# Memory's sums in 116 columns, six low halves on GpSimd, and a new order, in a gated attention and feed-forward kernel

## The chip, the cores and the metric

The kernel runs on one core of a Trainium2 chip. The metric is device time in microseconds (us), the median of several executions. The engines are TensorE (PE in the profile, its weight loads PEld), VectorE (DVE), ScalarE (ACT), GpSimd (POOL), and SyncE (SP), whose queue issues most transfers.

## The reference

One input `x` of 2048 tokens by 448 features goes through two branches that share it, and a gate mixes them:

```python
g = _sigmoid((x * gate_w).sum(-1, keepdims=True))
a = _A_ref(x, A_wq, A_wk, A_wv, A_wo, A_beta)
b = _B_ref(x, B_w1, B_w2)          # silu(x @ w1) @ w2, 448 -> 1792 -> 448
return g * a + (1 - g) * b
```

Branch A is attention with 16 heads of 28 features in four segments of 512 tokens. Inside a segment it is ordinary causal attention. Across segments there is a memory, a 28 x 28 matrix M and a vector z for each head:

```python
for s in range(N):
    qs, ks, vs = q[:, :, s], k[:, :, s], v[:, :, s]
    ...                             # a_dot: causal softmax attention
    pq = phi(qs)                    # phi(t) = t + 1 if t > 0 else exp(t)
    num = jnp.einsum("bhld,bhde->bhle", pq, M)
    den = jnp.einsum("bhld,bhd->bhl", pq, z)[..., None] + 1e-6
    o = g * num / den + (1.0 - g) * a_dot
    pk = phi(ks)
    M = M + jnp.einsum("bhld,bhle->bhde", pk, vs)
    z = z + jnp.einsum("bhld->bhd", pk)
```

## The kernel before

**Precision.** Matmuls run on 16-bit numbers, but every operand is kept as two halves: a high half (the scaled value rounded to 16 bits) and a low half (the scaled value less the high one). A product takes three matmuls: high by high, high by low, low by high. The high half is mostly made by ACT (L603), the low half by `rest`: one DVE instruction (L592), or two POOL instructions (L594 scales in place, L595 subtracts).

**Stages.** `project()` covers about the first 155 us. It loads x and the weights, finds scales, splits x and the weights into halves, makes queries, keys (`proj`) and values (`vproj`) for 16 groups `t` (segment `s`, four heads `g` each), and builds and reads the memory (`memory`, `retrieve`). Attention (`attention`) and a first pass of the feed-forward branch (ten of 14 blocks) follow together; the second pass and the output projection end the kernel. The queries and keys go through DRAM (`q_scr`, `k_scr`) and come back as `ring`.

**x's halves.** `xhalves(s, c, prio)` makes both halves of segment `s`'s chunk `c`: four chunks of features, the last one with 64 rows. For the first segment DVE makes the low halves. For the others the planner chooses DVE or POOL; in the profile all of them are on DVE.

**Memory.** There are 12 units: `memory(t, ...)` for segments 0 to 2. PE adds, over four blocks of 128 tokens, phi(k)'s halves by v's halves in one PSUM tile: the first matmul (L1046) takes phi(k)'s high half by both halves of v, 232 columns; the second (L1048) phi(k)'s low half by v's high half, 116 columns. DVE adds the two column sets together (L1057, into `md`). POOL multiplies by `bds` (L1060), which holds scales and zeros where a key's head isn't the value's, and, from segment 1 on, adds into `macc` (L1062). ACT and POOL split `macc` into `mhl` (L1065, L1066), which `retrieve` uses as a matmul operand (L1083, L1084) for the next segment.

**Scales.** After the scale of a segment's x is known (`top`, `up`), POOL makes a chain of small operations: `true` and `kscale`, then `others`, which makes `bds` (`PREADY`) and then the scales of the scores (`EREADY`).

**Order.** `tc.manual_schedule()` is on, and the order of all instructions comes from a planner written in the kernel (`Sched`). Every task has an engine (or two to choose from), an estimated duration, dependencies, buffers that it takes, and a priority. The planner lets the tasks run in its own model, always the one that can start first, and among those that can start at the same time the one with the lowest priority number; that fixes each engine's program. For PE, `price` adds a cost for weight loads that wouldn't be hidden. Group `t` of the projections has priority 10 t in `project()`; attention's head `n` has 10 n, and the feed-forward's first pass is spread from `FLO` to `FHI`. About 45 constants shift these priorities: `OT1` places `others`, `SS` a segment's x halves, `MP` memory, `FIRST` and `MAXO` the first attention group, `WPRIO` and `XPRIO` the feed-forward's weights and scales, `WOT` and `WOP` the output projection, `LOP` the low halves of attention's weights. `few(n, ...)` tells the planner that a POOL task takes 0.33 n us. `MORE` is the number of extra warm-up matmuls that PE may run when it has nothing else (L816).

Of the kernel before, what the change touches and what calls it, by code (L numbers as in the profile page):

```python
# [14 lines left out]
OP = mybir.AluOpType  # L15
AX = mybir.AxisListType
# [4 lines left out]
GW = 4 * DH  # L21
# [5 lines left out]
TB = L // 128  # L27
SCALE = DH ** -0.5
LIFT = 8.0 * math.log(2.0)
TALL = 2.0 ** 15  # L30
NEG = -1.0e30
NT = NSEG * NG
NH = NT * 4
NA = 5
COLD = 5.0
WARM = 8
MORE = 4
HPRIO = 30.66
BANKS = {"mm": 3, "sc": 3, "cc": 2}
FREE = FB - 1  # L40
PASSES = [list(range(0, 10)), list(range(10, FB))]
# [3 lines left out]
DOWN = 2.0 ** -19  # L45
TINY = 2.0 ** -40
FIT = 2.0 ** -15
WOT = 286.86
TUS = 1.6
TLAT = 4.0  # L50
SLACK = -0.5
LOP = 75.43
LATE = -0.33
FIRST = 111.83
WPRIO = 120.5
MAXO = 65.16
FULL = 0.111
LOCK = 0.06
RB = "cc"
MP = 26.33  # L60
VF = -48.01
VA = 10.9
VS = 2.57
NV = 8
XH0 = -43.53
NF = 4
VE = 6.87
LASTQ = 5.78
WQS = -110.77
VH = 48.29  # L70
XS0 = -70.23
VC = -7.5
OT1 = -83.52
XS = 36.84
QS = -38.93
KS1 = -37.16
SS = -17.65


def VP(o, k):  # L80
    return o + VA + VS * k if o or k > VF else -1.0 + 0.1 * k


PRICE = 303.25
PRICE2 = 1.93
SLACK2 = 0.6
PVRUNS = [((1, 0), 1)]
PVP = 47.73
FLO = 57.98
FHI = 686.35  # L90
WOP = 120.98
SZ = 17.27
SZSTEP = -0.26
XPRIO = 311.22
WBP = 41.87
XLEAD = 146.82


# [180 lines left out]
def infini_mix(ctx: ExitStack, tc: tile.TileContext, x, wq, wk, wv, wo, beta, w1, w2, out):  # L279
    nc = tc.nc  # L280
# [39 lines left out]
    def half(cols, n=1):  # L320
        return [(0.0025 + cols * 0.000418, 0.027)] * n
# [15 lines left out]
    def dve(cols, fn, *deps, **k):  # L337
        return sch.add("DVE", 0.07 + 0.00104 * cols, fn, deps, **k)
# [4 lines left out]
    def pool(cols, fn, *deps, **k):  # L343
        return sch.add("POOL", 0.1 + 0.0019 * cols, fn, deps, **k)
# [33 lines left out]
    WV, WQ, HQ, WK, HK, W1, W2, WO, NS = range(NSEG, NSEG + 9)  # L378
# [50 lines left out]
    SIZE, SQUARED, SCALED, XH, JUNK = {}, {}, {}, {}, []  # L429
# [92 lines left out]
    def few(n, fn, *deps, **k):  # L522
        return sch.add("POOL", 0.33 * n, fn, deps, port=None, **k)
# [26 lines left out]
    def others(s, prio, bds, own, t_own, t_gh):  # L550

        def mem():
            z = spk[:, NSEG + s:NSEG + s + 1]
            by(z, top[:, WK:WK + 1], top[:, xi(s)], 1.0 / FIT)
            by(z, z, 1.0 / UP, op0=OP.max)
            by(bds[:, s, :, DH:], own[:, :, None], z[:GW])
            by(bds[:, s, :, :DH], own[:, :, None].to_broadcast([GW, 4, DH]), z[:GW], rv[:GW, s:s + 1])

        def go():
            by(rv[:, s:s + 1], top[:, WV:WV + 1], top[:, xi(s)], 1.0 / FIT)  # L560
            by(omgs[:, s], omg, rv[:, s:s + 1])
# [12 lines left out]
        EREADY[s] = few(8, scores, PREADY[s], SCALED[WQ], SCALED[WK], prio=prio + 0.5)  # L574
        END1.append(EREADY[s])

    DER = {}
# [188 lines left out]
    def project():  # L766
# [82 lines left out]
        def xhalves(s, c, prio):  # L849
            ALL, END = slice(None), slice(REM, 128)  # L850
            b, d = XR.pop((s, c))
            if s == 0:
                sl = slice(c * 128, (c + 1) * 128)
                hi = (ALL, slice(0, 4), sl)
                lo = [((ALL, slice(4, 7), sl), (ALL, slice(0, 3)), (ALL, slice(0, 3), sl)),
                      ((END, NC, sl), (END, NC), (END, NC, sl))]

                def src():
                    return b.v.rearrange("p (c n) -> p c n", c=4)
            else:  # L860
                hi = (ALL, c)
                lo = [((ALL, 4 + c), (ALL,), (ALL, c)) if c < NC else ((END, NC), (END,), (END, NC))]

                def src():
                    return b.v
            XC[s, c] = halves(NSEG - 1 - s, hi, lo, lambda: X16[s], src, L, d, prio, uses=[b], both=s == 0,
                              on="DVE" if s == 0 else None)
            XH.setdefault(s, []).extend(XC[s, c])

        XC, EARLY = {}, {}  # L870
# [164 lines left out]
        def memory(t, prio):  # L1035
            s, g = divmod(t, NG)
            b, done = PK.pop(t)
            ps = Buf(BK["cc"])
            vs = [VB[s * TB + tb] for tb in range(TB)]

            def go():
                p = ps.v[:GW, :2 * (GW + 4)]
                q = p.rearrange("p (h t e) -> p h t e", h=4, t=2)
                for tb in range(TB):
                    vv = vs[tb][0].v[:, 4 * g:4 * g + 4]
                    nc.tensor.matmul(p, b.v[:, 0, tb], vv.rearrange("p h t e -> p (h t e)"), start=(tb == 0), stop=False,  # L1046
                                     skip_group_check=True)
                    nc.tensor.matmul(q[:, :, 0], b.v[:, 1, tb], vv[:, :, 0], start=False, stop=(tb == TB - 1),  # L1048
                                     skip_group_check=True)
            m = pe((half(232) + half(116)) * TB, go, *done, *[d for v in vs for d in v[1]], takes=[ps],  # L1050
                   uses=[b] + [v[0] for v in vs], prio=prio)
            ma = macc[:, g].rearrange("p (h e) -> p h e", h=4)
            d = Buf(R["md"])

            def red():
                p = ps.v[:GW, :2 * (GW + 4)].rearrange("p (h t e) -> p h e t", h=4, t=2)
                nc.vector.tensor_reduce(d.v, p, axis=AX.X, op=OP.add)  # L1057

            def acc():
                nc.gpsimd.tensor_mul(ma if s == 0 else d.v, d.v, bds[:, s])  # L1060
# [46 lines left out]
        for i in range(4):  # L1107
            b = Buf(WAR)
# [412 lines left out]
```

## Time and profile before

| | |
|---|---|
| median of 3 runs | 550.92 us (549.62 to 553.25) |
| the profiled execution | 551.97 us |
| its span, first to last instruction | 550.0 us |
| mean granted clock of TensorE | 0.997 |
| bytes moved by DMA | 78.93 MB |

The profile is of one execution. Its page gives busy times by engine and the chain of work that ended last. Other views group instructions by line, list them in time, or give the busy time of each engine in a stretch of time. A row of the timeline has its start, its duration (or the stretch from the first to the last of several), engine, line, operation, output and inputs, shape and count; what stands in brackets is the idle time of that engine before it and what ended it. A matmul's duration in a row is its whole way through the array; how often a new one starts tells what it costs.

### The profile page before, as it was taken

What the parts mean: (1) busy time and instruction counts of PE and PEld (TensorE: products, weight loads), DVE (VectorE), ACT (ScalarE), POOL (GpSimd) and SP (SyncE); (2) the same over time, 40 slices, a digit from 0 to 9 for tenths busy, and PEclk for the clock granted to TensorE, in tenths of its full rate; (3) what the DMA queues carried; (4) which work ended last, traced back from release to release, by engine and by line L of the source; (5) the groups of instructions that cost most, each with busy time, mean ns of one, the idle gap of its engine ahead of it and who ended that gap; (6) DMA issues with size and microseconds to landing.
All of it is one profiled execution on the core that took longest, in us unless ns stands there. A gap on an engine that the chain in (4) does not pass through costs nothing.

```text
span 550.0 us, 11589 instructions
## 1 busy us (share of the span) xinstructions
PE 538.9 (98%) x4027; PEld 299.0 (54%) x4027; DVE 409.7 (74%) x1003; ACT 408.0 (74%) x698; POOL 357.6 (65%) x551
## 2 busy tenths in 40 slices
PE   8999999999998999999999999999999999999997
PEld 3445556665634555555565556565555555555544
DVE  4999899988759877598665889877888137654473
ACT  5978899687347988899887998889999897410140
POOL 3356353676515878998799998899889996122210
PEclk9999999999999899999999999999999999999999
DMA  8769786346457242432324334356402222699872
GB/s 277 257 201 247 225 241 202 129 118 200 144 161 199 80 113 72 150 88 70 85 86 120 87 89 122 103 137 179 81 12 65 86 69 65 228 243 240 235 163 73
DMA packets 78058, 78.93 MB, mean 144 GB/s; under 512 B 44168, under 2 KB 67720, under 8 KB 78000
## 3 DMA queue, kind: packets, MB, share of 16 engines
q1 hardware_dynamic: 77424, 77.21, 49.2%
q10 hardware_dynamic: 576, 0.99, 0.6%
q8 instruction: 31, 0.51, 0.4%
q14 instruction: 27, 0.22, 0.2%
HBM read 48.41 MB, written 26.09 MB: 135 GB/s over the span
## 4 chain that ended last, share of the span: by engine, by line
PE 84%; DMA 5%; DVE 5%; ACT 3%; issue 1%; SPq 1%; POOL 0%; DVEq 0%; ACTq 0%; POOLq 0%
PE mm L629 23%; PE mm L1235 17%; PE sc L629 10%; PE sc L734 6%; PE sc L1331 6%; PE cc L1365 6%; PE cc L1235 6%; PE cc L629 5%; DMA rawf<-in_w_dram 2%; PE sc L992 2%; DMA raw<-in_wv_dram 1%; ACT pf L1336 1%; PE cc L1083 1%; DMA ring<-k_scr 1%; DMA xraw<-in_x_dram 1%
## 5 line engine op out<-in xcount | busy, mean ns | idle before, releaser
L1352 POOL TENSOR_TENSOR phl<-pf,phl 128x384 f16<-128x384 f32 (+1 forms) x192 | 187.3, 997 | 14.6 <-ACT phl L1348 13.7
L1336 ACT ACTIVATE pf<-sc,lift,es 128x512 f32<-128x512 f32 (+1 forms) x192 | 125.9, 708 | 8.9 <-PE sc L1331 8.0
L747 DVE CUSTOM_DVE_ANT_0 sc<-sc,mk 128x384 f32<-128x384 f32 (+1 forms) x192 | 105.2, 572 | 25.6 <-PE sc L734 22.4
L1235 PE MATMUL mm<-wb,ghl 128*128 128x448 f16 (+2 forms) x516 | 112.6, 348 | 0.2 <-DVE wb L592 0.2
L629 PE MATMUL mm<-xh,wa 128*128 128x512 f16 x429 | 108.2, 378 | 0.0
L1235 PEld LDWEIGHTS <-ghl 128*128 128x128 f16 x684 | 63.9, 97 | 51.9 <-issue 0.8
L1348 ACT ACTIVATE phl<-pf 128x1280 f16<-128x1280 f32 x64 | 80.8, 1272 | 12.0 <-POOL pf L1342 11.5
L629 PEld LDWEIGHTS <-wa 128*128 128x128 f16 x572 | 54.0, 98 | 55.7 <-issue 3.8
L1331 PE MATMUL sc<-ring 86*128 86x512 f16 (+3 forms) x256 | 61.9, 300 | 0.2
L734 PE MATMUL sc<-ring 84*128 84x128 f16 (+3 forms) x256 | 59.4, 300 | 2.4 <-DMA ring<-k_scr 1.4
L1373 DVE TENSOR_REDUCE oraw<-cc 128x116 f32<-128x232 f32 x64 | 25.3, 395 | 28.8 <-PE cc L1365 28.6
L1365 PEld LDWEIGHTS <-phl 128*128 128x128 f16 x1280 | 41.4, 96 | 8.9
L1365 PE MATMUL cc<-vg,phl 128*128 128x29 f16 (+1 forms) x1280 | 43.6, 182 | 0.0
L629 PE MATMUL mm<-xh,wks 128*128 128x512 f16 x176 | 43.0, 380 | 0.4 <-DVE stg L934 0.4
L640 POOL TENSOR_TENSOR ol<-ol,ml 128x448 f32<-128x448 f32 x12 | 14.1, 1172 | 44.5 <-DMA ol<-o_scr 25.1
L629 PE MATMUL mm<-xh,wqs 128*128 128x512 f16 x176 | 42.0, 379 | 0.4 <-DVE vt L1016 0.4
L629 PE MATMUL cc<-xh,wa 128*128 128x512 f16 x143 | 37.7, 389 | 0.6 <-DVE amr L1089 0.4
L1235 PE MATMUL cc<-wb,ghl 128*128 128x448 f16 x168 | 38.2, 352 | 0.0
L1342 POOL TENSOR_SCALAR_AFFINE_SELECT pf<-pf 128x384 f32<-128x384 f32 x64 | 33.7, 527 | 6.6 <-ACT pf L1336 6.0
L646 ACT ACTIVATE oh<-ol,os 128x448 f16<-128x448 f32 x16 | 10.7, 666 | 34.7 <-POOL ol L640 34.7
L1331 PEld LDWEIGHTS <-ring 86*128 86x128 f16 x256 | 24.0, 97 | 22.7 <-issue 1.5
L629 PE MATMUL sc<-wos,oT 128*128 128x448 f16 x176 | 35.4, 352 | 0.0
(190 smaller groups left out, 943.0 us busy)
## 6 DMA issues: line engine op xcount, KB each, us to landing
rawf<-in_w_dram SPq DMA_DIRECT2D x26, 256.0 KB
rawf<-in_w_dram SPq DMA_DIRECT2D x28, 224.0 KB
v_scr<-vt SPq DMA_DIRECT2D x16, 232.0 KB
vg<-v_scr SPq DMA_DIRECT2D x16, 232.0 KB
xraw<-in_x_dram SPq DMA_DIRECT2D x14, 256.0 KB
q_scr<-stg SPq DMA_DIRECT2D x16, 224.0 KB
ring<-q_scr SPq DMA_DIRECT2D x16, 224.0 KB
k_scr<-stg SPq DMA_DIRECT2D x16, 224.0 KB
```

What stands on the lines that cost most here:

```text
L629: nc.tensor.matmul(ps(), *p[i], start=(i == 0), stop=(i == n - 1))
L640: d = pool(530, lambda: nc.gpsimd.tensor_add(b.v, b.v, m.v), d, e, uses=[b, m], **k)
L734: nc.tensor.matmul(ps.v[:, u:u + n], rg.v[:KS, 0, hh, i * 128:(i + 1) * 128], rg.v[:KS, 1, hh, :n], start=i + t > 0, stop=(i + t > 0 or j ...
L747: nc.vector.tensor_tensor_reduce(r, r, MK[:, L - n:], 1.0, NEG, OP.add, OP.max, mx.v[:, hh, i:i + 1])
L1235: nc.tensor.matmul(ps.v[:, lo:hi], g.v[:, y, sl], w.v[:, z, lo:hi], start=(j == 0 and i == 0), stop=(j == len(fs) - 1 and i == 2))
L1331: nc.tensor.matmul(ps.v[:, e:e + w], rg.v[:KK, 1, hh, j * 128:(j + 1) * 128], rg.v[:KK, 0, hh, j * 128:], start=True, stop=True)
L1336: ex.append(sact(e, lambda b=b, ps=ps, pf=pf, e=e: nc.scalar.activation(pf.v[:, b, :e], ps.v[:, :e], AF.Exp, bias=lift, scale=es[:, s:s + ...
L1342: mk.append(pool(204, lambda pf=pf: nc.gpsimd.affine_select(pf.v[:, :, :128], pf.v[:, :, :128], [[0, 3], [1, 128]], OP.is_ge, 0.0, base=0, ...
L1348: hi = copy(1280, lambda hl=hl, flat=flat: nc.scalar.activation(hl.v[:, 0], flat(), AF.Copy), *mk, takes=[hl], uses=[pf], prio=p0 + 2)
L1352: low = pool(w - u + 22, lambda hl=hl, flat=flat, u=u, w=w: nc.gpsimd.tensor_sub(hl.v[:, 1, u:w], flat()[:, u:w], hl.v[:, 0, u:w]), low, u ...
L1365: nc.tensor.matmul(p[:, i, :2 - z], hl.v[:, z, u:u + 128], vg.v[:, j, hh, :2 - z], start=(z == zs[0] and i == 0), stop=(z == zs[-1] and j ...
L1373: nc.vector.tensor_reduce(orw.v[:, hh], p, axis=AX.X, op=OP.add)
```

## The change

Three things are changed, and the planner's constants with them.

1. `memory`: three matmuls of 116 columns for each block of tokens, all into the same 116 columns of PSUM, take the place of one of 232 and one of 116. DVE multiplies that sum, read from PSUM, by `bds`; there is no reduction, and POOL's multiplication is gone. For segment 0 DVE writes `macc` itself; later POOL adds `md` into it.
2. `xhalves`: for segments 1 to 3 the low halves of chunks 0 and 2 are made by POOL, in two instructions each. For chunks 1 and 3 the planner still chooses.
3. `MORE` goes from 4 to 6, and the planner's estimate of the last scale operations from 8 to 10 units of 0.33 us.

```diff
+AWAY = (0, 2)
...
-MORE = 4
-HPRIO = 30.66
+MORE = 6
+HPRIO = 11.4
...
-WOT = 286.86
+WOT = 458.77
...
-LOP = 75.43
-LATE = -0.33
-FIRST = 111.83
-WPRIO = 120.5
-MAXO = 65.16
+LOP = 190.26
+LATE = -0.25
+FIRST = 169.25
+WPRIO = 82.91
+MAXO = 73.19
...
-MP = 26.33
+MP = 23.77
...
-OT1 = -83.52
...
-SS = -17.65
+OT1 = -132.99
...
+SS = -14.27
...
-PRICE2 = 1.93
-SLACK2 = 0.6
+PRICE2 = 250.34
+SLACK2 = -0.07
...
-FLO = 57.98
-FHI = 686.35
-WOP = 120.98
+FLO = 15.0
+FHI = 718.21
+WOP = 60.65
...
-XPRIO = 311.22
-WBP = 41.87
+XPRIO = 190.9
+WBP = 14.98
...
-        EREADY[s] = few(8, scores, PREADY[s], SCALED[WQ], SCALED[WK], prio=prio + 0.5)
+        EREADY[s] = few(10, scores, PREADY[s], SCALED[WQ], SCALED[WK], prio=prio + 0.5)
...
-                              on="DVE" if s == 0 else None)
+                              on="DVE" if s == 0 else "POOL" if c in AWAY else None)
...
             def go():
-                p = ps.v[:GW, :2 * (GW + 4)]
-                q = p.rearrange("p (h t e) -> p h t e", h=4, t=2)
+                p = ps.v[:GW, :GW + 4].rearrange("p (h e) -> p h e", h=4)
                 for tb in range(TB):
                     vv = vs[tb][0].v[:, 4 * g:4 * g + 4]
-                    nc.tensor.matmul(p, b.v[:, 0, tb], vv.rearrange("p h t e -> p (h t e)"), start=(tb == 0), stop=False,
-                                     skip_group_check=True)
-                    nc.tensor.matmul(q[:, :, 0], b.v[:, 1, tb], vv[:, :, 0], start=False, stop=(tb == TB - 1),
-                                     skip_group_check=True)
-            m = pe((half(232) + half(116)) * TB, go, *done, *[d for v in vs for d in v[1]], takes=[ps],
+                    for i, (y, z) in enumerate(((0, 0), (0, 1), (1, 0))):
+                        nc.tensor.matmul(p, b.v[:, y, tb], vv[:, :, z], start=tb + i == 0, stop=tb == TB - 1 and i == 2)
+            m = pe(half(116) * 3 * TB, go, *done, *[d for v in vs for d in v[1]], takes=[ps],
                    uses=[b] + [v[0] for v in vs], prio=prio)
             ma = macc[:, g].rearrange("p (h e) -> p h e", h=4)
             d = Buf(R["md"])
 
-            def red():
-                p = ps.v[:GW, :2 * (GW + 4)].rearrange("p (h t e) -> p h e t", h=4, t=2)
-                nc.vector.tensor_reduce(d.v, p, axis=AX.X, op=OP.add)
-
-            def acc():
-                nc.gpsimd.tensor_mul(ma if s == 0 else d.v, d.v, bds[:, s])
-                if s > 0:
-                    nc.gpsimd.tensor_add(ma, ma, d.v)
-            r = dve(227, red, m, takes=[d], uses=[ps], prio=prio)
-            r = pool(156 if s == 0 else 423, acc, r, PREADY[s], *MH.get((s - 1, g), []), uses=[d], prio=prio)
+            def mul():
+                p = ps.v[:GW, :GW + 4].rearrange("p (h e) -> p h e", h=4)
+                nc.vector.tensor_mul(ma if s == 0 else d.v, p, bds[:, s])
+            r = dve(150, mul, m, PREADY[s], *(MH.get((s - 1, g), []) if s == 0 else []), takes=[d] if s else [], uses=[ps], prio=prio)
+            if s:
+                r = pool(156, lambda: nc.gpsimd.tensor_add(ma, ma, d.v), r, *MH.get((s - 1, g), []), uses=[d], prio=prio)
```

The constants left out of this diff move in the same way: `XH0`, `VF`, `VA`, `VS`, `VE`, `VH`, `LASTQ`, `WQS`, `XS0`, `XS`, `QS`, `KS1`, `PRICE`, `PVP`, `SZ` and `SZSTEP`.

More of the change, by code (lines that the diff above doesn't have):

```diff
@@ L59 @@
 RB = "cc"
-MP = 26.33
-VF = -48.01
-VA = 10.9
-VS = 2.57
+MP = 23.77
+VF = -58.98
+VA = 12.89
+VS = 2.6
 NV = 8
-XH0 = -43.53
+XH0 = -65.85
 NF = 4
[L67 to L71, printed above, removed]
-VC = -7.5
-OT1 = -83.52
-XS = 36.84
-QS = -38.93
-KS1 = -37.16
-SS = -17.65
+VE = 6.88
+LASTQ = 5.69
+WQS = -96.81
+VH = 16.89
+XS0 = -38.95
+VC = -7.5
+OT1 = -132.99
+XS = 34.38
+QS = -42.27
+KS1 = -18.8
+SS = -14.27
 def VP(o, k):
     return o + VA + VS * k if o or k > VF else -1.0 + 0.1 * k
-PRICE = 303.25
-PRICE2 = 1.93
-SLACK2 = 0.6
+PRICE = 290.47
+PRICE2 = 250.34
+SLACK2 = -0.07
 PVRUNS = [((1, 0), 1)]
-PVP = 47.73
-FLO = 57.98
-FHI = 686.35
-WOP = 120.98
-SZ = 17.27
-SZSTEP = -0.26
-XPRIO = 311.22
-WBP = 41.87
+PVP = 49.52
+FLO = 15.0
+FHI = 718.21
+WOP = 60.65
+SZ = 11.47
+SZSTEP = 0.05
+XPRIO = 190.9
+WBP = 14.98
 XLEAD = 146.82
```

## The prediction

> **What bounds the kernel now.** I read the page first: its busy times, and the shares of the chain that ended last. After it the busy times by stretch, then the timeline of each engine where the edits lie.
>
> ```profile
> span 550.0 us, 11589 instructions
> ...
> PE 538.9 (98%) x4027; PEld 299.0 (54%) x4027; DVE 409.7 (74%) x1003; ACT 408.0 (74%) x698; POOL 357.6 (65%) x551
> ...
> PE 84%; DMA 5%; DVE 5%; ACT 3%; issue 1%; SPq 1%; POOL 0%; DVEq 0%; ACTq 0%; POOLq 0%
> ```
>
> TensorE (PE) is busy for all but 550.0 - 538.9 = 11.1 us, and 84% of the chain is its own work. Whatever the other engines save is worth only what it takes out of these 11.1 us, plus what it takes out of a slowed clock. Where do they lie? In the view by stretch the columns are PE, PEld, DVE, ACT, POOL, granted clock, DMA share and GB/s:
>
> ```profile
> 20.00:40.00 20.00, 19.16 (x89) 8.48 (x88) 19.76 (x40) 16.13 (x36) 8.82 (x13) 1.00 0.70 213
> 40.00:60.00 20.00, 19.92 (x126) 11.77 (x124) 19.51 (x37) 16.25 (x42) 10.75 (x27) 1.00 0.89 246
> ...
> 160.00:180.00 20.00, 17.24 (x84) 7.78 (x83) 15.77 (x39) 13.57 (x23) 8.64 (x10) 0.95 0.69 185
> 180.00:200.00 20.00, 19.90 (x176) 11.06 (x175) 16.16 (x43) 18.94 (x29) 16.27 (x23) 0.96 0.28 76
> ```
>
> The handover from the projections to attention (160 to 200) holds 2.76 + 0.10 = 2.86 us of idle PE, and a granted clock of 0.95 and 0.96 there, worth another 20 x 0.05 + 20 x 0.04 = 1.8 us. From 20 to 60 us VectorE (DVE) is busy for 39.27 of 40 us beside an almost full PE. So DVE is the second bound just where the edits fall, and GpSimd (POOL), at 19.57 of 40 us, has room.
>
> **The change part by part.** The profiled execution took 551.97 us with its span of 550.0, so 1.97 us lie around the span; the median of the runs shown is 550.92, 1.05 lower. I make the sum on 551.97 and carry it over to the median with that difference.
>
> *Memory's matmuls.* There are 12 units of four blocks. A block was one matmul of 232 columns and one of 116; now it is three of 116. Start to start in the PE timeline gives their price:
>
> ```profile
> 42.42 0.26 PE L1046 MATMUL cc<-vt,phk 128*112 128x232 f16 x1
> 42.52 0.22 PE L1048 MATMUL cc<-vt,phk 128*112 128x116 f16 x1
> 42.57 0.26 PE L1046 MATMUL cc<-vt,phk 128*112 128x232 f16 x1
> ```
>
> The 232 columns take 0.10 us (42.42 to 42.52), the 116 take 0.05 (42.52 to 42.57): 0.15 us a block before, 3 x 0.05 = 0.15 after. The rows are rounded to 0.01 us, so three of them may be 0.015 off either way, times 48 blocks: 0 +- 0.7 us. I take +0.2.
>
> *Two more warm-up matmuls (MORE 4 to 6).* Two of the four run just ahead of the row at 5.81, two at 20.65 in the same timeline:
>
> ```profile
> 5.81 0.99 PE L992 MATMUL sc<-raw,xraw 128*128 128x450 f32 x2 [0.95 <-DMA xraw<-in_x_dram]
> ...
> 20.65 0.60 PE L816 MATMUL mm<-maskb 128*128 128x512 bf16 x2
> 21.09 4.91 PE L629 MATMUL mm<-xh,wqs 128*128 128x512 f16 x22
> ```
>
> Such a matmul costs (21.09 - 20.65) / 2 = 0.22 us. In the 0.95 us of idle PE ahead of 5.81 two of them cost nothing; at 20.65, in front of the first projection, they cost 0.44. I take the middle, +0.2.
>
> *Memory's sums.* The reduction on DVE and the masking on POOL become one multiplication on DVE that reads PSUM.
>
> ```profile
> L1057 DVE TENSOR_REDUCE md<-cc x12: 383/390/394, 45.0 to 143.1; 112x116 f32<-112x232 f32 x12
> L1060 POOL TENSOR_TENSOR md<-md,bds x8: 428/433/878, 80.6 to 143.6; 112x116 f32<-112x116 f32 x8
> ```
>
> ```profile
> L759 DVE SCALAR_TENSOR_TENSOR mhl<-sc,mhl x16: 268/274/279, 98.4 to 431.2; 16x128 f16<-16x128 f32 x16
> ```
>
> The new operation is in no row. From above the old reduction of twice the columns bounds it (0.390 us), from below the nearest DVE row with one input in PSUM and one in SBUF (0.274 for 128 columns); I take 0.27, since the row's size is almost the same. DVE gains 12 x 0.12 = 1.4 us, POOL 12 x 0.43 = 5.2 us. A wait is added: DVE's multiplication now waits for POOL's mask (bds), and behind it in DVE's order stand the second halves of projections (stg), which free PE's banks. The first mask is ready at 42.64 (row 42.21 below) and the first reduction ran at 45.0, so this wait is covered by 2.4 us, if POOL makes the mask no later.
>
> *Low halves of x's chunks 0 and 2, segments 1 to 3.* Six of the nine full DVE operations go to POOL, which needs two passes for each.
>
> ```profile
> L592 DVE SCALAR_TENSOR_TENSOR xh<-xraw,up,xh 128x512 f16<-128x512 f32 x9 | 6.3, 744 | 0.0
> ```
>
> ```profile
> 169.92 1.57 POOL L594 TENSOR_SCALAR rawf<-rawf,up 128x512 f32<-128x512 f32 x1
> 171.57 1.15 POOL L595 TENSOR_TENSOR wa<-rawf,wa 128x512 f16<-128x512 f32 x1
> ```
>
> DVE gains 6 x 0.744 = 4.5 us; POOL pays 6 x (1.57 + 1.15) = 16.3 us. POOL's sum is then 357.6 + 16.3 - 5.2 = 368.7 us, still no bound as a sum. What matters is when PE asks for these halves. For segment 1 (PE, then ACT, then POOL):
>
> ```profile
> 43.03 0.73 PE L629 MATMUL sc<-wvs,xh 128*128 128x450 f16 x3
> ...
> 45.27 1.69 PE L629 MATMUL sc<-wvs,xh 128*128 128x450 f16 x8
> ```
>
> ```profile
> 36.96 0.72 ACT L603 ACTIVATE xh<-xraw,up 128x512 f16<-128x512 f32 x1
> ```
>
> ```profile
> 42.21 0.43 POOL L529 TENSOR_SCALAR bds<-of,spk,rv 112x112 f32<-112x112 f32 x1
> ...
> 49.19 0.22 POOL L527 TENSOR_SCALAR wide<-wide 128x1 f32<-128x1 f32 x1
> ```
>
> Chunk 0's high half ends at 37.68. If POOL takes both low halves at once, they end at 37.7 + 2.72 = 40.4 and 43.1. PE asks for chunk 0 at 43.03 and for chunk 2 only within the eight matmuls from 45.27: nothing is lost. If they stand behind the first mask (42.64), they end at 45.4 and 48.1, and PE is 2.4 us late. If they stand behind the whole chain of small scale operations (to 49.41), see the rival. Between the first two I take half, +1.2. For segment 2:
>
> ```profile
> 68.92 2.85 DVE L592 SCALAR_TENSOR_TENSOR xh<-xraw,up,xh 128x512 f16<-128x512 f32 x4
> ```
>
> ```profile
> 80.35 0.81 PE L629 MATMUL mm<-xh,wqs 128*128 128x512 f16 x3
> ```
>
> DVE was done at 71.77 and the query projection first asks at 80.35: 8.6 us of cover, which holds even 3 x 2.72 us of POOL. I cost it at nothing; the cover is gone only if POOL starts after 74.9.
>
> *What DVE's 5.9 us can buy.* Of PE's waits in the stretch, DVE ended three:
>
> ```profile
> 26.36 2.54 PE L629 MATMUL mm<-xh,wqs 128*128 128x512 f16 x11 [0.35 <-DVE vt L1016]
> ...
> 29.96 4.91 PE L629 MATMUL mm<-xh,wks 128*128 128x512 f16 x22 [0.42 <-DVE stg L934]
> ...
> 66.74 0.73 PE L629 MATMUL sc<-wvs,xh 128*128 128x450 f16 x3 [0.40 <-DVE vt L1016]
> ```
>
> Together 0.35 + 0.42 + 0.40 = 1.17 us; the first two lie ahead of every operation that is taken from DVE. So between 0 and 1.17 is gained; I take -0.5.
>
> *The redrawn order.* About forty constants of the planner move the places of nearly all work, and the profile shows none of it. Downward it can win no more than the handover and those waits (2.86 + 1.8 + 1.17 = 5.8); upward, one more place like the handover costs 4.7. I take 0 and keep both ends.
>
> Sum: 0.2 + 0.2 + 1.2 - 0.5 + 0 = +1.1, so the profiled execution would take 551.97 + 1.1 = 553.1 us, and the median 1.05 less: 552.0 us. The rivals below are priced from the median at once.
>
> *A rule on the port.* In this trace DVE and POOL hold each other up. One DVE operation of the low-half kind took 1.59 us while POOL was in its subtractions:
>
> ```profile
> 217.62 1.59 DVE L592 SCALAR_TENSOR_TENSOR wb<-rawf,up,wb 128x448 f16<-128x448 f32 x1
> ```
>
> ```profile
> 216.70 2.03 POOL L1352 TENSOR_TENSOR phl<-pf,phl 128x384 f16<-128x384 f32 x2
> ```
>
> ```profile
> L592 DVE SCALAR_TENSOR_TENSOR wb<-rawf,up,wb x12: 672/735/1646, 175.5 to 460.4; 128x448 f16<-128x448 f32 x12
> ```
>
> The median of its kind is 0.735 and the longest 1.646, so one meeting costs up to 0.91 us. The Trainium skill, "SBUF — State Buffer", section "Who interferes with whom", says that a DVE instruction with two SBUF inputs and a GpSimd instruction that reads SBUF exclude each other, the second waiting until the first is through; the rows agree. It speaks against this change: twelve new POOL passes read SBUF beside a DVE that is full. What that would make of the time is the third rival.
>
> **The rivals.**
>
> *Faster: the handover closes.* With 5.9 us less on DVE the projections end earlier, and the new order has no wait and no slow clock at 160 to 200. For it: DVE's 39.27 of 40 us. Against it: that handover shows a DVE that is busy only 15.77 of 20 us, so it is not DVE that it lacks. It gives 550.9 - 5.8 = 545.1 us.
>
> *Slower: POOL's order.* The place is segment 1's chunk 0. If POOL runs its chain of small operations first, to 49.41, chunk 0's low half ends at 49.41 + 2.72 = 52.1, against the 43.03 at which PE asks: 9.1 us. PE's work from 43.60 to 45.27 can go ahead of it, 1.7 us, which leaves 7.4. It decides from the point where chunk 0's low half ends after 43.03 + 1.7 = 44.7. For it: the planner gives most of that chain the better priority (segment 1's part of it stands at 40 + OT1 = 40 - 132.99 = -93, the halves at 30 + SS = 16, and the lower goes first). Against it: the planner sees the same durations and would price such a wait. It gives 550.9 + 0.4 + 7.4 = 558.7.
>
> *Slower: the port.* If each of the twelve POOL passes meets a DVE operation with two SBUF inputs, DVE loses 12 x 0.91 = 10.9 us against 5.9 gained, 5.0 net, in stretches where it has no slack; with the 2.4 us of lateness above, 550.9 + 0.4 + 7.4 = 558.7 as well. For it: the row of 1.59 us. Against it: most DVE operations there read PSUM or a single tile.
>
> **How the numbers follow.** Forecast 0.43, handover closes 0.20, POOL's order 0.22, port 0.15. About 1%, 5.5 us, is what a measurement of this kernel can tell from no change: the within-1% band is 545.4 to 556.4, and the forecast with its unknowns (-5.8 to +4.7 around 552.0) lies in it but for its ends. So faster 0.20, same 0.43, slower 0.37. The forecast's own range is 547 to 556. The range for 8 in 10 goes from 544.5, just under the faster rival, to 561, the slower ones with the uncertain 2 us of their sums.
>
> **What would show it.** Memory's three matmuls: start to start 0.05 us. DVE's multiplication: 0.27 us, no reduction left. POOL's low halves: 2.7 us a chunk, and their end against the first PE operation on segment 1. DVE's busy time from 20 to 110 us some 4 to 6 us lower. The port: DVE operations on L592, or those that read two tiles, over 1 us beside POOL's passes. The handover: idle PE and granted clock at 160 to 200. I am wrong if PE idles over 3 us near 43 us, or if the idle time at the handover is under 1 or over 6 us.

## The result, and the profile after

| | median | range | n | ratio to before [95% interval] |
|---|---|---|---|---|
| before | 551.71 us | 549.62 to 556.52 | 13 | |
| after | 548.79 us | 548.16 to 550.68 | 13 | 0.9949 [0.9928, 0.9970] |

The changed kernel is 0.5% faster, between 0.3% and 0.7%: 2.9 us where the prediction's sum had +1.1. The page after, its span, busy times and chain of waits:

```profile
span 547.0 us, 11704 instructions
...
PE 538.3 (98%) x4077; PEld 300.0 (55%) x4077; DVE 408.4 (75%) x1004; ACT 406.7 (74%) x696; POOL 359.4 (66%) x543
...
PE 86%; ACT 5%; DMA 4%; DVE 2%; issue 1%; SPq 1%; DVEq 0%; ACTq 0%
```

PE's idle time fell from 11.1 to 547.0 - 538.3 = 8.7 us. DVE's sum fell by 1.3 us only, although 5.9 us of work were taken from it: the planner put other work there, in part what POOL had (two low halves of the weights `wvs` and two sums `hsum`, 1.35 and 1.84 us on DVE). By stretch, with the columns of before:

```profile
20.00:40.00 20.00, 20.00 (x100) 9.69 (x100) 19.76 (x42) 16.49 (x37) 4.55 (x8) 1.00 0.81 253
40.00:60.00 20.00, 19.66 (x120) 10.86 (x119) 18.45 (x35) 18.98 (x47) 18.66 (x32) 1.00 0.87 256
160.00:180.00 20.00, 17.10 (x86) 8.02 (x84) 17.83 (x47) 13.52 (x21) 10.52 (x12) 0.91 0.56 153
180.00:200.00 20.00, 19.71 (x198) 11.54 (x196) 18.07 (x46) 19.21 (x32) 16.26 (x24) 1.00 0.33 95
```

From 20 to 40 us PE has no idle time left, and POOL is now nearly full from 40 to 60. The handover is as it was: 2.90 + 0.29 us of idle PE. Over the stretches ahead of it, before and then after:

```profile
0.00:20.00 20.00, 17.85 (x49) 7.66 (x50) 11.99 (x48) 13.35 (x36) 5.96 (x31) 1.00 0.85 280
20.00:150.00 130.00, 128.22 (x753) 74.26 (x752) 119.19 (x250) 99.72 (x221) 71.12 (x144) 1.00 0.65 193
```

```profile
0.00:20.00 20.00, 18.96 (x51) 7.76 (x52) 12.77 (x49) 14.44 (x38) 6.13 (x31) 1.00 0.80 283
20.00:150.00 130.00, 129.66 (x811) 75.78 (x811) 116.78 (x252) 99.46 (x220) 79.28 (x142) 1.00 0.65 195
```

PE's idle time falls from 2.15 to 1.04 us up to 20 us, and from 1.78 to 0.34 us from 20 to 150. (A second profile of before, *before_again* below, has 1.56 and 1.64.) The first feed-forward matmul, before and then after:

```profile
150.93 2.32 PE L629 MATMUL cc<-xh,wa 128*128 128x512 f16 x10 [0.37 <-DVE amr L1089]
```

```profile
148.46 2.54 PE L630 MATMUL cc<-xh,wa 128*128 128x512 f16 x11
```

The first of attention's scores come 20.45 us after it in before (171.38) and 20.55 us after it in the changed kernel (169.01). So in these profiles 2.4 of the 3.0 us by which the span is shorter are gained in the projections, ahead of the handover. The edits themselves, in the timelines of PE and POOL and in the rows of DVE's line:

```profile
42.79 0.81 PE L1047 MATMUL cc<-vt,phk 128*112 128x116 f16 x12
43.44 0.81 PE L630 MATMUL mm<-xh,wqs 128*128 128x512 f16 x3
44.09 2.26 PE L630 MATMUL sc<-wvs,xh 128*128 128x450 f16 x11
```

```profile
39.02 1.57 POOL L595 TENSOR_SCALAR xraw<-xraw,up 128x512 f32<-128x512 f32 x1 [0.72 <-ACT xh L604]
40.67 1.16 POOL L596 TENSOR_TENSOR xh<-xraw,xh 128x512 f16<-128x512 f32 x1
...
44.76 1.58 POOL L595 TENSOR_SCALAR xraw<-xraw,up 128x512 f32<-128x512 f32 x1
46.43 1.16 POOL L596 TENSOR_TENSOR xh<-xraw,xh 128x512 f16<-128x512 f32 x1
```

```profile
L1055 DVE TENSOR_TENSOR md<-cc,bds x8: 259/270/279, 75.5 to 136.5; 112x116 f32<-112x116 f32 x8
```

Twelve matmuls of 116 columns take 43.44 - 42.79 = 0.65 us. Chunk 0's low half of segment 1 ends at 41.83, PE asks for it at 44.09. DVE's multiplication takes 0.27 us. So each edit does what it says, at the forecast price. The rows show where PE waits less, but not which of the edits, or the new order, did it.

### The profile page after: what moved, and what is told of

Read it like the earlier page. It is cut to its first block, busy times and chain, and to the rows that moved or that the text cites. A ratio compares the mean times of both kernels' runs of the same rounds, so it can differ in the third digit from the quotient of the medians.

```text
span 547.0 us, 11704 instructions
## 1 busy us (share of the span) xinstructions
PE 538.3 (98%) x4077; PEld 300.0 (55%) x4077; DVE 408.4 (75%) x1004; ACT 406.7 (74%) x696; POOL 359.4 (66%) x543
## 4 chain that ended last, share of the span: by engine, by line
PE 86%; ACT 5%; DMA 4%; DVE 2%; issue 1%; SPq 1%; DVEq 0%; ACTq 0%
PE mm L630 25%; PE mm L1229 16%; PE sc L630 10%; PE sc L735 6%; PE sc L1325 6%; PE cc L630 6%; PE cc L1229 6%; PE cc L1359 6%; DMA rawf<-in_w_dram 2%; PE sc L993 2%; ACT pf L1330 2%; PE cc L1047 1%; PE cc L1077 1%; ACT phl L1342 1%; PE sc L977 1%
## 5 line engine op out<-in xcount | busy, mean ns | idle before, releaser
L1229 PE MATMUL mm<-wb,ghl 128*128 128x448 f16 (+2 forms) x516 | 110.8, 348 | 0.0
L735 PE MATMUL sc<-ring 84*128 84x128 f16 (+3 forms) x256 | 58.3, 300 | 2.5 <-ACT pf L1330 2.3
```

Source lines behind the costliest of these rows:

```text
L735: nc.tensor.matmul(ps.v[:, u:u + n], rg.v[:KS, 0, hh, i * 128:(i + 1) * 128], rg.v[:KS, 1, hh, :n], start=i + t > 0, stop=(i + t > 0 or j ...
L1229: nc.tensor.matmul(ps.v[:, lo:hi], g.v[:, y, sl], w.v[:, z, lo:hi], start=(j == 0 and i == 0), stop=(j == len(fs) - 1 and i == 2))
```

## The experiments

Each run stands beside runs of before on the same chip; ratios are to those.

**Order and edits taken apart.** *edits_alone* is the changed code with all constants of before; *order_alone* the code of before with the constants of after:

```diff
-HPRIO = 11.4
+HPRIO = 30.66
...
-XH0 = -65.85
+XH0 = -43.53
```

> The changed code (three matmuls of 116 columns, DVE's masking, low halves of chunks 0 and 2 on GpSimd, MORE 6, 10 units) with all 33 constants of the kernel before. Theory A, the edits themselves give the gain, because they relieve VectorE where it is full: 548 to 550 us, TensorE's idle time from 20 to 160 us falls from 2.2 us to under 1, and the projections (up to the first feed-forward matmul) end some 2 us sooner than 150.9. Theory B, the gain is in the redrawn constants: 551 to 553 us, and the projections end at 150 to 152. Theory C, the constants were fitted to each kernel, so that either half alone is worse than both kernels: over 553 us.

> The code before (MORE 4, 8 units) with all 33 constants of the changed kernel. Theory A: 551 to 553 us, the projections end no sooner than 150.5 us. Theory B: 548 to 550 us, the projections end at about 148.5. Theory C: over 553 us.

Measured: edits_alone 569.28 us, 1.0316 [1.0288, 1.0344]; order_alone 555.91, 1.0053 [1.0030, 1.0077]. Neither half is the gain; the edits in the old constants cost 17 us. There the prediction's rival on POOL's order came true. The timeline of POOL in edits_alone, then the one of PE:

```profile
40.38 0.26 POOL L530 TENSOR_SCALAR rv<-top 128x1 f32<-128x1 f32 x1
...
50.13 0.22 POOL L528 TENSOR_SCALAR wide<-wide 128x1 f32<-128x1 f32 x1
50.32 1.58 POOL L595 TENSOR_SCALAR xraw<-xraw,up 128x512 f32<-128x512 f32 x1
51.99 1.15 POOL L596 TENSOR_TENSOR xh<-xraw,xh 128x512 f16<-128x512 f32 x1
```

```profile
53.19 0.81 PE L630 MATMUL mm<-xh,wqs 128*128 128x512 f16 x3 [3.32 <-POOL xh L596]
```

Twenty-odd small operations stand ahead of chunk 2's low half, and PE waits 3.3 us for it. That is about a fifth of the 17 us, and the longest wait is another one, 6.5 us for DVE's pp.

**Single edits taken back out of the changed kernel**, the planner drawing the order anew: *away_none* leaves every low half to the planner's choice, *old_memory* has memory's old form.

```diff
-AWAY = (0, 2)
+AWAY = ()
```

> The changed kernel, but no low half is forced to GpSimd (AWAY empty; the planner chooses again). If the low halves on GpSimd are what relieves VectorE (4.5 of the 5.9 us), TensorE waits again for VectorE between 20 and 160 us and the time is 550.5 to 552 us. If they are worth nothing, it stays at 548.5 to 549.5. If they cost something (port, later halves), it falls under 548.3.

> The changed kernel with memory's old form (232 and 116 columns, reduction on VectorE, multiplication on GpSimd). If the new form of memory gives the gain, the time is 550.5 to 552 us; if it is worth nothing on the path, 548.5 to 549.5; the old form's matmuls take TensorE 0.2 to 0.4 us less in all, so 548.2 to 548.6 if that is all that counts.

Measured: away_none 549.43 us, 0.9949 [0.9930, 0.9968], the ratio of the change itself: the six low halves on POOL are worth nothing that the intervals can tell. Its PE is idle for 0.03 us from 20 to 150 us:

```profile
20.00:150.00 130.00, 129.97 (x812) 75.90 (x812) 118.82 (x257) 99.08 (x223) 61.84 (x130) 1.00 0.66 195
```

So it isn't the low halves that close PE's waits there. As for old_memory, it took 564.78 us, 1.0227 [1.0199, 1.0256]. That need not be memory's price, since the planner drew another order for it.

**The planner held still.** To leave the order of before as it is, *held_memory* keeps the planner's tasks and durations of before and changes only what memory's tasks issue. *new_memory* is the same edit with the planner told of it. *held_more* is the changed kernel with two of its six extra warm-up matmuls issuing nothing. *edits_xraw12* is edits_alone with 12 buffers for x instead of eight, after a wait for such a buffer had been seen at 53 us.

```diff
 def red():
-    nc.vector.tensor_reduce(d.v, p, axis=AX.X, op=OP.add)
+    nc.vector.tensor_mul(ma if s == 0 else d.v, p, bds[:, s])
 def acc():
-    nc.gpsimd.tensor_mul(ma if s == 0 else d.v, d.v, bds[:, s])
     if s > 0:
         nc.gpsimd.tensor_add(ma, ma, d.v)
```

> The kernel before with memory's new instructions (three matmuls of 116 columns, VectorE's multiplication by bds from PSUM, no multiplication on GpSimd), while the planner still sees the old tasks and costs, so that every instruction keeps its place. It has VectorE 1.4 us and GpSimd 5.2 us shorter and TensorE 0.2 to 0.4 us longer. Theory order (the edit is worth nothing by itself): ratio 0.998 to 1.002. Theory edit (relief of VectorE moves the path): ratio 0.997 or less, that is 1.5 us or more.

> The kernel before with memory's new form as the change has it, planned anew with the constants of before; low halves, MORE and the scale tasks as before. If the low halves on GpSimd are what spoiled the edits under the old constants (569.3 us), this stays within 549 to 554 us. If memory's form did it, over 560 us.

> The changed kernel with two of the six warm-up matmuls left out (tasks 2 and 3 of the planner issue nothing), every other instruction in its place. If the two cost their 0.22 us each ahead of the first projection: 548.3 us, ratio 0.994. If they lie in time that TensorE would wait anyway: 548.8, ratio 0.995. If they keep the clock up for what follows: over 549.5.

> The changed code with the constants of before (569.3 us) and 12 instead of 8 buffers for x, so that segment 3's loads don't wait for the buffers of segment 1. Theory queue: there SyncE stood 5.1 us at such a load until GpSimd's low half had freed its buffer, with all later loads and stores behind it; with the buffers that wait is gone, TensorE's waits of 3.3 and 6.5 us at 53 and 65 us shrink to under 3 us together, and the time falls to 550 to 558 us. Theory late half: TensorE simply lacks the low halves that GpSimd makes late; then the time stays over 564 us.

| run | median | ratio [interval] |
|---|---|---|
| held_memory | 549.19 us | 0.9944 [0.9919, 0.9970] |
| new_memory | 557.52 us | 1.0100 [1.0068, 1.0131] |
| held_more | 550.19 us | 0.9953 [0.9925, 0.9981] |
| edits_xraw12 | 572.83 us | 1.0368 [1.0315, 1.0422] |

Memory's edit alone, in the unchanged order, gains as much as the whole change. The same edit with a new order loses 1.6% against it: what an order drawn anew does by itself is several times the effect under study, and old_memory, new_memory and edits_alone can't be read as prices of edits. held_more can't be told from the change, so the two warm-ups cost nothing measurable: without them the first projection starts at 20.45 us instead of 20.84, and PE then waits 0.7 us for DVE. More buffers for x don't help.

The change and held_memory reach nearly the same time, but not in the same way. In held_memory the first feed-forward matmul starts at 150.22 us, only 0.7 us sooner than in before, and PE is still idle for 1.46 us from 20 to 150 us; the first of attention's scores then come 18.7 us after it, 1.7 us sooner than in before. In the changed kernel it is the other way round: 2.5 us by the first feed-forward matmul, and nothing between it and the scores. So what is found out below about memory's edit in the old order need not be what the changed kernel gains by.

**Whose relief is it?** On held_memory's base, *held_pool* gives POOL its multiplication back and lets DVE only copy the sum; *held_dve* loads DVE with a copy ahead of its multiplication; *held_form* has three matmuls of 116 columns while DVE reduces 232 elements (each sum taken twice, the larger kept) and POOL multiplies, so that no engine is relieved. *before_again* is before, profiled once more.

```diff
 # held_form
+    nc.vector.tensor_reduce(d.v, p[:, :, :, None].to_broadcast([GW, 4, DH + 1, 2]), axis=AX.X, op=OP.max)
 def acc():
+    nc.gpsimd.tensor_mul(ma if s == 0 else d.v, d.v, bds[:, s])
```

> Like held_memory (the program of before in its old order, memory's sums by three matmuls of 116 columns), but with the old division of labour: VectorE only copies the sum out of PSUM (some 0.27 us in place of the reduction's 0.39) and GpSimd multiplies by the mask again (0.43 us, twelve times). Theory GpSimd: the gain of held_memory (549.2 beside 552.0) comes from the multiplication that GpSimd no longer has, which stands in the chain sum, macc, mhl, retrieve, am, and so ahead of the loads that the first scores wait for; then this run falls back to 551 to 552.5. Theory VectorE: the gain comes from the twelve shorter VectorE operations, or from the matmuls; then this run stays at 548.5 to 549.7.

> Like held_memory, with one more VectorE operation in each of the twelve units: a copy of the sum into md (some 0.27 us) ahead of the multiplication, so that VectorE is busy for about 0.54 us a unit, 0.15 more than before the change, while GpSimd keeps its relief. Theory VectorE: it costs more than the whole gain, 552 to 554. Theory GpSimd: little is lost, 549 to 550.

> The kernel before once more, unchanged: a second profile. If the waits that held_memory lacks (PE for stg and vt near 66 us, PE for the load of k_scr at 165 us) belong to the program, they stand here again, of the same length to 0.2 us, and the first scores start at 171.4 to within 0.5 us. If they are chance of one execution, they don't.

> Only the form of the matmuls: three of 116 columns in the order of before, while VectorE keeps a reduction over 232 elements (the larger of each sum and itself, read twice; 0.39 us) and GpSimd keeps its multiplication. So neither engine is relieved. The matmuls themselves took 0.65 us a unit beside 0.61, 0.4 us more in all. Theory relief (either engine's will do, since held_pool and held_dve both kept some 2 us of the gain): back at the time before or a little over, 551.5 to 553. Theory start (with three matmuls the first loads land some 0.5 us earlier and the rest runs as before): 551 to 552. Theory form (the gain hangs on the program with three matmuls, whatever VectorE and GpSimd do): 549 to 550.3.

The rows of memory's tile md show in held_dve a DVE with 0.27 + 0.28 us a unit, and in held_form the old durations on both engines:

```profile
L1054 DVE COPY md<-cc x12: 260/267/279, 44.6 to 143.0; 112x116 f32<-112x116 f32 x12
L1055 DVE TENSOR_TENSOR md<-cc,bds x8: 278/278/279, 80.1 to 143.3; 112x116 f32<-112x116 f32 x8
```

```profile
L1054 DVE TENSOR_REDUCE md<-cc x12: 384/390/396, 44.0 to 142.5; 112x116 f32<-112x232 f32 x12
L1057 POOL TENSOR_TENSOR md<-md,bds x8: 429/433/879, 79.7 to 142.9; 112x116 f32<-112x116 f32 x8
```

| run | median | ratio [interval] |
|---|---|---|
| held_pool | 549.85 us | 0.9960 [0.9939, 0.9982] |
| held_dve | 549.53 us | 0.9956 [0.9937, 0.9976] |
| held_form | 549.64 us | 0.9953 [0.9933, 0.9974] |

All three keep most of the gain, held_form too, at the time that the theory of form gave. So in this order relief is not what gives most of the gain, though a share of 0.1 to 0.2% (0.9944 beside 0.9953 to 0.9960) isn't excluded. What is left is the form: 144 matmuls where there were 96, whose own time is not shorter but 0.04 us a unit longer. The second profile of before has the same wait as the first at the handover: PE for the load of k_scr, 1.4 us in one and 1.7 us in the other; its waits near 62 to 67 us are of other lengths.

**Instructions that compute nothing.** What else do 48 more matmuls bring? With their weight loads, 96 more instructions on TensorE. The page's list of DMA queues shows a kind "instruction": queue q8 in before, and in held_memory:

```profile
q8 instruction: 31, 0.51, 0.4%
```

```profile
q8 instruction: 32, 0.52, 0.4%
```

These are transfers of 0.51 MB / 31 = 16 KB, about one for 260 of TensorE's 2 x 4027 matmuls and weight loads, and with 96 more there is one more. So they are read here as the fetching of TensorE's program; the kernels below bear this out, where 48 and 96 more instructions bring the transfer at 158.2 us forward by 4.8 and 10.1 us, and 256 more bring the one behind it to 157.7. The Trainium skill, "Runtime: NRT & Kernel Launch", section "Instruction fetch mechanics", says that an engine's program is refilled in blocks of 16 KiB, 256 instructions, and calls the cost "mostly hidden". The size and the step agree with the rows; whether it is hidden is what the next runs measure. Seen beside the timeline of SP's queue, which issues the loads, before has one of these transfers in 157 to 160 us:

```profile
q8 instruction: 1, 0.02, 2.2%
```

```profile
157.14 1.04 SPq L364 DMA_DIRECT2D rawf<-in_w_dram  x2
158.23 1.46 SPq L364 DMA_DIRECT2D ring<-q_scr  x1
159.74 0.80 SPq L364 DMA_DIRECT2D ring<-k_scr  x2
```

It starts at 158.2 and takes 1.05 us, and the load issued at that moment occupies the queue for 1.46 us. In the other profile of before the transfer starts at 158.1 and the same issue takes 1.76. In held_memory, held_pool, held_dve and held_form the transfer comes at 147.8 to 148.7, and the issue takes 0.41.

Four kernels move these transfers and leave all work behind the warm-ups as it is. The eight warm-up matmuls of 512 columns at the start, where PE has no other work, are cut into more and shorter ones: 24 more (*pad_less*), 48 more (*padded*, as many as memory's new form adds), and 128 more, a whole block of 256 instructions (*pad_block*), all in the code of before; and 87 more in the changed kernel (*after_shift*).

```diff
 # padded
-    wb.v, maskb, maskb[:, None, :].to_broadcast([128, 4, 128]), start=True, stop=True) for _ in range(WARM)],
+    wb.v[:, :72], maskb, maskb[:, :72], start=True, stop=True) for _ in range(WARM + 48)],
```

> The kernel before, whose eight warm-up matmuls of 512 columns are cut into 56 of 72 columns: 48 more instructions for TensorE, as many as memory's new form adds, in a place where it has no other work. In the profiles so far the first matmul on x starts at 5.8 to 6.1 us in every program with memory's old form (4 of 4) and at 5.2 to 5.4 in every one with the new form (9 of 9), although the loads are issued at the same moment to 0.01 us. Theory length of the program: the first matmul on x starts at 5.2 to 5.45 us here too, and the time falls by 0.3 to 0.7 us. If only memory's own form does it: 5.8 us, and the time before.

> The kernel before with 128 more warm-up matmuls (136 of 30 columns in place of eight of 512), which are 256 more instructions of TensorE with their weight loads. The profile's instruction queue q8 moves 16 KB at a time, about once in 256 instructions of TensorE. In both profiles of before one such transfer starts at 158.1 to 158.2 us and takes 1.05 to 1.41, and at the same moment SyncE's issue of ring<-q_scr takes 1.46 to 1.76 us in place of 0.41, ahead of the loads for the first scores. In padded and in the four programs with memory's new form in the old order it starts at 147.8 to 148.7 and the issue takes 0.41. With a whole block of 256 added, the transfers fall where they fell in before. Theory transfer: one stands at 157.5 to 158.5 again, the issue takes 1.2 us or more, the first scores start 20.3 to 20.8 us after the first feed-forward matmul, and of the gain of padded (3.9 us) at least 1 is lost: 550 to 551.6. Theory length: any longer program is as fast as padded, 548 to 549.3.

> The changed kernel with 87 more warm-up matmuls (95 of 43 columns in place of eight of 512), 174 more instructions of TensorE. In the changed kernel q8's transfers start at 144.5 and 176.5 us and the issue of ring<-q_scr stands at 153.4; the shift puts a transfer at 152.5 to 154.5. Theory transfer: the issue of a load in 152 to 156 us takes over 1 us, the first scores come 0.7 to 1.5 us later against the first feed-forward matmul (20.55 us after it now), and the time is 549.5 to 551 in place of 548.8: the gain of the change is undone in part by instructions that compute nothing. If the transfers don't matter: 548.3 to 549.3.

> The kernel before with 24 more warm-up matmuls (32 of 128 columns), 48 more instructions of TensorE: half the shift of padded. The transfer that starts at 158.2 us in before (TensorE's instruction 1696 of the trace) comes at about 153, between SyncE's issues at 150.2 and 155.2, where nothing is issued. Theory transfer: every issue of a ring load in 150 to 160 us takes under 0.9 us a row (0.41 for the one at 157.5 to 158.2), the first scores come 18.7 to 19.8 us after the first feed-forward matmul, and the time is that of padded, 548.3 to 549.8. Theory length (the gain grows with the program): half of padded's, 550 to 551. If padded was chance: 551.5 to 553.

| run | more matmuls | transfer near the handover | median | ratio [interval] |
|---|---|---|---|---|
| padded | 48 | 148.1 us | 548.54 us | 0.9924 [0.9897, 0.9951] |
| pad_less | 24 | 153.4 us | 550.21 us | 0.9928 [0.9898, 0.9958] |
| pad_block | 128 | 157.7 us | 552.08 us | 0.9990 [0.9963, 1.0017] |
| after_shift | 87, in the changed kernel | 155.0 us | 550.37 us | 0.9960 [0.9936, 0.9983] |

The same rows of SP's queue in padded, pad_less and pad_block:

```profile
157.50 0.41 SPq L364 DMA_DIRECT2D ring<-q_scr  x1
```

```profile
158.86 0.41 SPq L364 DMA_DIRECT2D ring<-q_scr  x1
```

```profile
157.69 1.56 SPq L364 DMA_DIRECT2D ring<-q_scr  x1
```

And the load of one_scr in the changed kernel, then in after_shift, where the transfer was put on it:

```profile
154.71 0.85 SPq L365 DMA_DIRECT2D ring<-one_scr  x3
```

```profile
155.16 2.43 SPq L365 DMA_DIRECT2D ring<-one_scr  x3
```

The slow issue goes where the transfer goes, in both kernels. In padded, with the transfer at 148.1 us, the store that is issued then is slow; in before and in padded:

```profile
149.13 0.45 SPq L364 DMA_DIRECT2D h_scr<-stg  x1
```

```profile
148.40 1.48 SPq L364 DMA_DIRECT2D h_scr<-stg  x1
```

So where the transfer stands on it, the loads of the keys are issued 1.0 to 1.4 us later: from the first feed-forward matmul to the issue of ring<-k_scr it takes 8.81, 9.11 and 8.91 us in before, before_again and pad_block, and 7.76 to 7.78 in padded, pad_less and the four held programs with the old order (held_memory, held_pool, held_dve, held_form). PE's first matmul on the loaded keys, in before, padded, pad_less and pad_block, with what it waited for:

```profile
164.97 0.82 PE L734 MATMUL sc<-ring 84*128 84x128 f16 x8 [1.37 <-DMA ring<-k_scr]
```

```profile
163.32 0.82 PE L734 MATMUL sc<-ring 84*128 84x128 f16 x8 [0.44 <-DMA ring<-k_scr]
```

```profile
164.73 0.82 PE L734 MATMUL sc<-ring 84*128 84x128 f16 x8 [0.49 <-DMA ring<-one_scr]
```

```profile
164.01 0.82 PE L734 MATMUL sc<-ring 84*128 84x128 f16 x8 [0.94 <-DMA ring<-k_scr]
```

The wait is 0.9 us shorter in padded and pad_less, and 0.4 us shorter in pad_block. But it doesn't follow from the issue alone. In held_form, where the issue is quick, PE waits longer than in pad_block, and held_dve has 1.20 us there:

```profile
164.03 0.82 PE L734 MATMUL sc<-ring 84*128 84x128 f16 x8 [1.03 <-DMA ring<-k_scr]
```

From the issue of ring<-k_scr to this matmul it takes 4.71 us in pad_block, 5.23 in before, 5.36 in padded, 5.94 in held_form and 6.12 in held_dve: the landing of the load varies by as much as the issue does, and why is open. So the later issue is shown, and its price for PE is not. In the times, padded and pad_less, 96 and 48 instructions longer than before, gain 0.7 to 0.8%; pad_block, longer still, gains nothing, and its interval doesn't touch theirs. So it isn't the length of the program by itself. Nor is it the granted clock, 0.997 in the mean of the runs of pad_less, of pad_block and of before beside each, and 0.998 in padded. That the place of the transfers does it is the reading that fits, but a rival stands: pad_block's warm-ups are the shortest, 136 of 30 columns, and its first projection starts late, at 21.46 us beside 21.09 in before. In its one profile that is made up by the first feed-forward matmul, 150.39 beside 150.93; but this execution took 549.70 us, 2.4 below the median of pad_block and less than the profiled one of padded (549.99), so it does not show where the others lose. The median of pad_less alone would fit a gain that grows with the length, but before stood at 553.22 us beside it, and the ratio is that of padded. Four expectations were missed: pad_less's median was put at that of padded, 548.3 to 549.8; padded's gain was put at 0.3 to 0.7 us and is 3.9; in pad_block the first scores come 19.80 us after the first feed-forward matmul (150.39 and 170.19) and not 20.3 or more, and its median is above what was expected; in after_shift the first scores are not late (20.60 us beside 20.55), since the slow issue is that of one_scr and not that of the first load. after_shift is not told apart from the change by its ratio (0.9960 beside 0.9949, intervals that overlap), though its slow issue is plain; for the changed kernel's own order the effect on the time stays unmeasured.

No other version beats the changed kernel by more than the measurement can tell; padded, which is before with its warm-up cut into pieces, equals it.

## Why the prediction was wrong, point by point

**The steps that failed.** The sum came out above zero because of one term, the low halves at +1.2; they cost nothing that the runs can tell (below), and without them it would have been -0.1. And the one gain that it took, -0.5 for PE's waits, is far from -2.9. In the profiles PE's idle time ahead of 150 us shrank by 1.11 + 1.44 = 2.6 us (by 1.8 against the second profile of before). The first part, the wait of 0.95 us for the first loads of x above all, was not in the sum at all; the second was mis-sized.

**A term that was missing: "0.15 us a block before, 3 x 0.05 = 0.15 after".** As a price on PE it held: 0.65 us a unit where 0.61 stood, 12 x 0.04 = 0.5 us beside the 0.2 taken. But it took the cost of a matmul to be its time in the array. The 48 more are also 96 more instructions, with their weight loads, and they shift all later transfers of TensorE's program. That term was not in the sum at all. The runs put it at -0.8% for a shift of 96 in the old order (padded), which is -2.7 to -5.7 us of 552.44, and held_memory, with the same count and the edit too, at no more than that. It can't be laid out by place: the profiles of before and padded differ by 1.92 us at PE's last end (546.25 - 544.33), but that of pad_block, whose median gains nothing, ends at 544.06. Nor is it shown that the changed kernel, with its order drawn anew, gains by this term.

**DVE's relief, -0.5 taken, 0 to -1.17 possible.** In the old order no gain from it could be measured: held_dve puts 0.15 us a unit more on DVE than before had, and held_form relieves neither engine; both are as fast as held_memory within the intervals. In the changed kernel the three waits are gone, and the idle time from 20 to 150 us is 1.44 us lower than in before, beyond the bound. The low halves' relief didn't do that, as away_none shows; order_alone, the new constants without the edits, has 3.09 us of idle PE there. So in these runs it takes edits and new order together, and no run parts memory's new sums from the order.

**Memory's sums.** The forecast of 0.27 us for the new operation, from the row of 128 columns, is what it takes. POOL's 0.43 us a unit are worth nothing measurable by themselves (held_pool).

**Low halves, +1.2 taken.** Too much: by away_none they are worth nothing that can be told. Chunk 0's low half came as soon as ACT's high half was there (the row at 39.02 shows 0.72 us of waiting for it), with most of the scale operations behind it, so it ends at 41.83, ahead of the 44.7 us from which the prediction let it decide. The price of a chunk, 2.7 us, was right.

**Warm-ups, +0.2 taken.** Nothing measurable: without two of them PE waits 0.7 us for DVE soon after (held_more).

**The order, taken at 0.** In the code of before the new constants cost 0.5%; in the changed code they save about 20 us against the old ones (edits_alone 569.28 us, the changed kernel 548.79). Its term can't be added to those of the edits: what the order gives is the repair of what drawing it anew would break.

**The rivals.** The handover did not close: its idle time is 3.19 us, beside 2.86 before, and its clock is 0.91 and 1.00. POOL's order came true only with the constants of before, at chunk 2 and at 3.3 us instead of 7.4. The port: in the changed kernel the longest DVE operation on x's low halves took 765 ns, with a mean of 748 for whole chunks, so none of them was held up by POOL's passes; the Trainium skill's rule ("SBUF — State Buffer", "Who interferes with whom") was not put to the test here.

**What stays open.** Which part of the change takes PE's waits out of the projections in the new order, and so what the changed kernel owes its 0.5% to. held_memory shows that memory's edit is enough for a gain of that size in the old order, and away_none and held_more that the other edits add none; but the gain lies at another place there, and after_shift, which moved a transfer onto a load, didn't measurably take it back. For the old order, why the time falls by more than the profiles place: other transfers of q8 also move, and no run placed them singly.

## What to carry to other kernels

Count the instructions that an edit adds to or takes from an engine, since here, on a nearly full engine, they moved the fetches of its program against the loads; an edit that gains half a per cent deserves a control that adds as many instructions and computes nothing. Where a planner draws the order, compare edits with the order held still: memory's edit gave -0.6% in the held order and +1.0% with the order drawn anew. And two kernels with the same time need not have it for the same reason: compare where their waits lie. A theory of relief is tested most cheaply by giving the relieved engine its work back.

## What the runs showed of the hardware

**Fetching a program isn't free.** A 16 KB transfer of q8 takes about 1 us (1.05 and 1.41 at the handover of before), and a load issued in that time held SyncE's queue for 1.46, 1.56, 1.76 and 2.43 us where 0.41 and 0.85 are usual. It isn't so each time: counted over all 18 traces of this case, 103 of the 283 issues of SyncE's queue that began during such a transfer took over 0.5 us more than the median of their kind, and 9 of the 6857 that met none.

**The first loads land earlier with a longer program.** They are issued at the same moment to 0.01 us. But PE's first matmul on x starts at 5.8 to 6.1 us in the two profiles of before, in order_alone and in old_memory, and at 5.2 to 5.6 in all fourteen programs that have 48 or more instructions of TensorE beyond them, here in before_again and in pad_less:

```profile
5.83 0.99 PE L992 MATMUL sc<-raw,xraw 128*128 128x450 f32 x2 [0.34 <-DMA xraw<-in_x_dram]
```

```profile
5.28 4.30 PE L992 MATMUL sc<-raw,xraw 128*128 128x450 f32 x8
```

In the changed kernel this goes with the idle time that PE loses ahead of 20 us (2.15 us, or 1.56 in the second profile of before, to 1.04). pad_block has the early start too (5.49 us) and gains nothing, so it isn't by itself what sets the time. No transfer of the kind "instruction" lies between 0.2 and 7 us in these traces; its cause is open.
